# Attention and a two-product layer on one core: from whole batches in turn to 384-token chunks in a pipeline

## The chip, the cores and the metric

The kernel runs on one core of one Trainium2 chip. The metric is the device time of one execution in microseconds (us), lower is better. Before the change three runs gave 482.09 us (median), 481.46 and 484.16 us.

## The reference

Causal attention over 4 batches, 8 heads, 768 tokens and 64 numbers per head. Three heads (0, 2 and 6, "retrieval") see every earlier token. The other five ("streaming") see the first 4 tokens (the sink) and the last 64. The heads' outputs, side by side, are rows of 512 numbers, and two products with a leaky ReLU between them follow.

```python
scores = scale * np.matmul(q, k.transpose(0, 1, 3, 2))
rel = pos[:, None] - pos[None, :]
causal = rel >= 0
in_win = (rel >= 0) & (rel < int(window))              # window = 64
stream_keep = causal & (is_sink | in_win)              # is_sink: pos < 4
mask = np.where(retr[0, :, 0, 0, None, None], full_mask, stream_mask)
scores = np.where(mask[None, :, :, :], scores, -1000000000.0)
a = np.exp(scores - np.max(scores, axis=-1, keepdims=True))
a = a / (np.sum(a, axis=-1, keepdims=True) + 1e-09)
x = np.matmul(a, v)             # then (4, 768, 8 * 64) -> (3072, 512)
h = x @ w_in                    # 512 x 2048
out = np.maximum(0.01 * h, h) @ w_out                  # 2048 x 512
```

All inputs and the output are float32.

## The kernel before, in words

One loop runs over the four batches of 768 tokens, and each batch goes through all its stages in turn. The tile framework's scheduler may move instructions of the next batch forward, as far as buffers allow.

**Weights.** Both matrices come in one DMA each of 4 MB, before most else, and ScalarE turns them into bf16 in one instruction each (L87, L92).

**Loads and transposes.** `qb`, `kb` and `vb` of a batch come in one DMA each (L111 to L113). ScalarE casts them to bf16 (L117, L125). Scores need the 64 numbers of a head on the partitions, so q and k are written to a bridge in DRAM (`qk_bridge`, L126) and read back by a transposing DMA (L130) as `qt` and `kt`. Two heads share a column of 128 partitions, 64 each.

**Attention**, head by head. For a retrieval head the scores of a block of 128 keys against all later queries go to PSUM (`psST`, L152, weights of 64 rows), ScalarE takes the exponential (`At`, L156), VectorE masks the diagonal block (L162), and TensorE multiplies with `vpad` (L166, 65 columns: 64 of v and one of ones, whose sum is the denominator). A streaming head does the same in blocks of 128 x 128 for the diagonal and for the block before it (L185, L190, L194, L198) and a product with 4 rows for the sink. A head's sums stay in `psO`, six banks of PSUM, in one buffer; L214 and L215 copy them out.

**Second bridge.** The whole batch is normalised at once (L220), written to DRAM (`x_bridge`, L227) and read back transposed as `xt` (L229).

**Both products**, for 512 and then 256 tokens: for each of 16 groups of 128 hidden columns four matmuls with `w_in_bf` (`psH`, L239), the leaky ReLU on ScalarE (`gT`, L245), and one matmul with `w_out_bf` per 128 tokens (`psOUT`, L249). L253 copies the result out, and one DMA per batch stores it (L254).

So TensorE runs attention of a batch, then its products, then attention of the next.

## Time and profile before

| | |
|---|---|
| median of 3 runs | 482.09 us |
| span of the profiled execution | 482.3 us |
| TensorE matmul busy | 316.1 us, 66% |
| ScalarE busy | 193.2 us, 40% |
| VectorE busy | 90.8 us, 19% |
| GpSimd busy | 13.9 us, 3% |

The profiled execution left no time besides its span, which is its first to its last instruction, and the span is 0.2 us above the median: nothing of note lies around it. PE is TensorE, PEld its weight load, ACT ScalarE, DVE VectorE, POOL GpSimd, SP the engine that issues the DMAs. A matmul's "mean ns of one" contains its latency: how fast matmuls follow each other is read from the starts of neighbouring rows of the timeline, or from n of them in a row as (time of the row - time of one) / (n - 1). [...] Before the first recorded change of the clock the rows show 1.00 throughout, also where TensorE had not run yet: the level of that stretch is read from the matmuls' spacing.

### The profile page before, as it was taken

To read this page: it belongs to the slowest core of one execution; us is meant where nothing else is said; L and a number is where in the kernel's file an instruction comes from. 1 tells how busy PE (TensorE), PEld (TensorE's weight loads), DVE (VectorE), ACT (ScalarE), POOL (GpSimd) and SP (SyncE) were. 2 spreads that over 40 slices of the span, in tenths; PEclk is the share of its full clock that TensorE was granted. 3 is DMA by queue.
4 is the path that set the end of the run, shared out by engine and by line. 5 is a ranking of instruction groups with operands and counts; after the bars stand their busy time and mean duration, and the time that the engine had idled before them with its cause. 6 is when DMAs were issued, how large, how long until landed. Compare 5 with 4: busy or idle time off the path is not lost.

```text
span 482.3 us, 4494 instructions
## 1 busy us (share of the span) xinstructions
PE 316.1 (66%) x1764; PEld 148.8 (31%) x1784; DVE 90.8 (19%) x234; ACT 193.2 (40%) x339; POOL 13.9 (3%) x22
## 2 busy tenths in 40 slices
PE   0000297720998888810999998807999889259992
PEld 0000044310334444400334444402345344124351
DVE  0000033350001043430001144330010433400011
ACT  1827165632435564520233465421333655012331
POOL 4000000020000000020000000020000000000000
PEclk9999999999999975555899965557999755559997
DMA  8999997189997030099000030192000300130003
GB/s 330 230 341 287 229 218 173 67 185 228 225 254 153 0 132 1 1 248 251 24 1 0 1 131 1 13 196 55 0 1 0 132 0 1 65 65 1 0 1 131
DMA packets 71029, 52.72 MB, mean 109 GB/s; under 512 B 37728, under 2 KB 65376, under 8 KB 70496
## 3 DMA queue, kind: packets, MB, share of 16 engines
q1 hardware_dynamic: 71008, 52.43, 43.5%
q8 instruction: 14, 0.23, 0.2%
q14 instruction: 7, 0.06, 0.0%
HBM read 27.26 MB, written 15.73 MB: 89 GB/s over the span
## 4 chain that ended last, share of the span: by engine, by line
PE 57%; DMA 20%; ACT 11%; issue 4%; DVE 3%; SPq 3%; ACTq 0%
PE psOUT L249 18%; PE psH L239 16%; PE psO L166 11%; PE psST L152 7%; DMA xt<-x_bridge 6%; DMA kb<-in_k_dram 5%; ACT At L190 5%; PE psST L185 5%; DMA x_bridge<-x_sb 4%; DMA qk_bridge<-tb 4%; ACT gT L245 3%; SPq L130 3%; DVE x_sb L220 1%; ACT tb L125 1%; ACT At L156 1%
## 5 line engine op out<-in xcount | busy, mean ns | idle before, releaser
L239 PE MATMUL psH<-xt,w_in_bf 128*128 128x512 bf16 (+1 forms) x508 | 102.2, 338 | 71.4 <-DMA xt<-x_bridge 69.8
L245 ACT ACTIVATE gT<-psH 128x512 bf16<-128x512 f32 (+1 forms) x128 | 62.0, 490 | 159.2 <-PE psH L239 154.3
L249 PE MATMUL psOUT<-w_out_bf,gT 128*128 128x512 bf16 x368 | 97.5, 391 | 7.1 <-ACT gT L245 4.9
L152 PE MATMUL psST<-qt,kt 64*128 64x512 bf16 (+4 forms) x116 | 45.3, 436 | 67.4 <-DMA kt<-qk_bridge 57.0
L239 PEld LDWEIGHTS <-w_in_bf 128*128 128x128 bf16 x512 | 51.2, 101 | 116.8 <-DMA xt<-x_bridge 70.4
L156 ACT ACTIVATE At<-psST 128x512 bf16<-128x512 f32 (+4 forms) x116 | 51.1, 472 | 46.0 <-PE psST L152 45.1
L166 PE MATMUL psO<-vpad,At 128*128 128x65 bf16 (+1 forms) x552 | 66.7, 234 | 2.9 <-DVE At L194 2.3
L253 DVE COPY out_sb<-psOUT 128x2048 f32<-128x2048 f32 (+1 forms) x8 | 14.1, 1758 | 233.6 <-PE psOUT L249 233.6
L166 PEld LDWEIGHTS <-At 128*128 128x128 bf16 (+1 forms) x552 | 37.9, 111 | 52.0 <-DVE At L162 18.9
L249 PEld LDWEIGHTS <-gT 128*128 128x128 bf16 x384 | 30.9, 99 | 59.0 <-ACT gT L245 35.3
L190 ACT ACTIVATE At<-psST 128x512 bf16<-128x512 f32 x80 | 32.7, 461 | 24.6 <-PE psO L166 13.3
L185 PE MATMUL psST<-qt,kt 64*128 64x128 bf16 x220 | 35.8, 288 | 8.7 <-ACT At L190 7.0
L152 PEld LDWEIGHTS <-kt 64*128 64x128 bf16 (+1 forms) x116 | 9.4, 97 | 74.0 <-DMA kt<-qk_bridge 57.0
L162 DVE TENSOR_TENSOR At<-At,m_caus 128x128 bf16<-128x128 bf16 x72 | 15.9, 225 | 86.0 <-ACT At L156 83.7
L185 PEld LDWEIGHTS <-kt 64*128 64x128 bf16 x220 | 19.8, 121 | 22.6 <-issue 18.8
L214 DVE COPY xu_sb<-psO 128x384 f32<-128x384 f32 x32 | 17.8, 558 | 44.2 <-PE psO L166 44.2
L116 POOL MEMSET vpad<- 128x3120 bf16 x4 | 10.8, 2698 | 301.6 <-PE psO L166 301.6
L117 ACT ACTIVATE vpad<-vb 128x3072 bf16<-128x3072 f32 x4 | 11.1, 2766 | 14.5 <-POOL vpad L116 14.5
L125 ACT ACTIVATE tb<-qb 128x3072 bf16<-128x3072 f32 x4 | 11.0, 2761 | 10.6 <-DMA qb<-in_q_dram 10.6
L220 DVE TENSOR_TENSOR x_sb<-xu_sb,linv 128x3072 bf16<-128x3072 f32 x4 | 13.4, 3358 | 0.1
L125 ACT ACTIVATE tb<-kb 128x3072 bf16<-128x3072 f32 x4 | 11.0, 2758 | 4.4 <-DMA kb<-in_k_dram 4.4
L87 ACT ACTIVATE w_in_bf<-wtmp 128x8192 bf16<-128x8192 f32 x1 | 7.0, 7029 | 11.5 <-DMA wtmp<-in_moe_w_in_dram 11.5
(26 smaller groups left out, 46.9 us busy)
## 6 DMA issues: line engine op xcount, KB each, us to landing
qk_bridge<-tb SPq DMA_DIRECT2D x8, 768.0 KB, 6.8
out_dram<-out_sb SPq DMA_DIRECT2D x4, 1536.0 KB, 5.9
wtmp<-in_moe_w_in_dram SPq DMA_DIRECT2D x1, 4096.0 KB, 12.8
wtmp<-in_moe_w_out_dram SPq DMA_DIRECT2D x1, 4096.0 KB, 18.2
...
qb<-in_q_dram SPq DMA_DIRECT2D x4, 0.2 KB, 11.7
...
```

The lines of the kernel that those rows point to most:

```text
L125: nc.scalar.activation(out=tb[:], in_=src[:], func=mybir.ActivationFunctionType.Copy)
L152: nc.tensor.matmul(psST[:krows, :ww], lhsT=kslab, rhs=Qth[:, qstart + off : qstart + off + ww], start=True, stop=True,)
L156: nc.scalar.activation(out=At[:krows, off : off + ww], in_=psST[:krows, :ww], func=mybir.ActivationFunctionType.Exp, scale=SM,)
L162: nc.vector.tensor_mul(At[:krows, :msk_end], At[:krows, :msk_end], msk[:krows, :msk_end])
L166: nc.tensor.matmul(psO[:, qi, : D + 1], lhsT=At[:krows, q_off : q_off + 128], rhs=Vph[:krows, kj, :], start=first[qi], stop=is_last,)
L185: nc.tensor.matmul(psST[:, i * 128 : i * 128 + 128], lhsT=Kth[:, kj * 128 : kj * 128 + 128], rhs=Qth[:, qi * 128 : qi * 128 + 128], start= ...
L190: nc.scalar.activation(out=At[:, g0 : g0 + len(grp), :], in_=psST[:, : len(grp) * 128], func=mybir.ActivationFunctionType.Exp, scale=SM,)
L214: nc.vector.tensor_copy(xu_sb[:, :, h, :], psO[:, :, :D])
L220: nc.vector.tensor_tensor(x_sb.rearrange("p cg (h d) -> p cg h d", h=H), xu_sb[:], linv.to_broadcast([128, NCG, H, D]), op=mybir.AluOpType ...
L239: nc.tensor.matmul(psH[:], lhsT=w_in_bf[:, fg, ng * 128 : ng * 128 + 128], rhs=xt[:, fg, tok0 : tok0 + T], start=(fg == 0), stop=(fg == NF ...
L245: nc.scalar.activation(out=gT[:], in_=psH[:], func=mybir.ActivationFunctionType.Prelu, alpha=0.01)
L249: nc.tensor.matmul(psOUT[:, tt, :], lhsT=gT[:, tt * 128 : tt * 128 + 128], rhs=w_out_bf[:, ng, :], start=(ng == 0), stop=(ng == NNG - 1),)
```

## The change

The program is rewritten. Tokens go in 8 chunks of 384, two per batch. The order of every engine is the order in which the code is written (`manual_schedule`).

- **Work lists.** `prep_slots`, `attention_slots`, `in_slots` and `out_slots` give lists of small pieces ("slots") of a chunk. `merge` issues them by turns: slots of chunk n's first product, of chunk n-1's second product and of chunk n+1's transposes and attention.
- **Order at the start.** Attention of chunk 0 alone, its first product alone, attention of chunk 1 alone, its first product alone; then the second product of chunk 0 with attention of chunk 2; from there for n = 2 to 6 three things together; then n = 7's first product with 6's second, and 7's second alone.
- **Transposes** of q, k and of the attention's output are bf16 matmuls against an identity into `pt` (one PSUM buffer) with a copy to SBUF behind them. Both DRAM bridges are gone.
- **Padded heads.** `kt` holds each head on all 128 partitions, zeros in the other head's half, so all matmuls have 128 rows. Streaming heads use windows of 128 keys per 64 queries; the sinks of all streaming heads share one product (`ksink`, `vs`).
- **Lag.** A unit's scores and exponential stand two slots ahead of its product with v.
- **Casts** of q, k and v move from ScalarE to GpSimd (chunk 0: k on VectorE, q on ScalarE); those of the weights go to VectorE and GpSimd in 16 pieces each, and weights are loaded in 8 DMAs of 1 MB. `vb` and `vs` are shifted copies of v, made by DMA within SBUF.
- **PSUM**: 2 buffers each for scores, `po` and `ph`; one each for `pt` and `py`.

What TensorE has in a row where products and attention meet. Before, at the end of a batch's attention (`psO` of the last head, then `psH` of the first hidden group):

```order
L166 LDWEIGHTS At_520
L166 MATMUL psO_502<-vpad_119,At_520 128x65
L166 LDWEIGHTS At_507
L166 MATMUL psO_502<-vpad_119,At_507 128x65
L239 LDWEIGHTS w_in_bf_105
L239 MATMUL psH_558<-xt_554,w_in_bf_105 128x512
```

Now, in the stage of n = 3, between two slots of the products (`ph` is the first product of chunk 3, `psS` and `po` are scores and sums of chunk 4):

```order
L350 LDWEIGHTS w_in_bf_113
L350 MATMUL ph_2060<-xt_1305,w_in_bf_113 128x384
L234 LDWEIGHTS kt0_99
L234 MATMUL psS_2066<-qt_1788,kt0_99 128x384
L198 LDWEIGHTS ats2_111
L198 MATMUL po_2071<-va0_101,ats2_111 128x65
```

Before, the two kinds meet once per batch; now a few matmuls of attention stand after every three or four of the products.

What SP issues at the start. Before, with the first batch's bridge in the sixth row:

```order
L86 DMA wtmp_107<-in_moe_w_in_dram 128x4x2048
L111 DMA qb_113<-in_q_dram 128x48x64
L112 DMA kb_114<-in_k_dram 128x48x64
L91 DMA wtmp2_110<-in_moe_w_out_dram 128x16x512
L113 DMA vb_115<-in_v_dram 128x48x64
L126 DMA qk_bridge<-tb_124 128x6x512
L126 DMA qk_bridge<-tb_128 128x6x512
L130 DMA_TRANSPOSE qt_122<-qk_bridge 128x4x768
```

Now, from the third quarter of `w_in` on (chunk 0 and two quarters stand ahead of these; `kf_419`, `qf_423`, `vf_427` are chunk 1, `kf_515` and its fellows chunk 2, `vb0` the shifted v of chunk 1):

```order
L73 DMA wf_381<-in_moe_w_in_dram 128x4x512
L73 DMA wf_393<-in_moe_w_in_dram 128x4x512
L67 DMA kf_419<-in_k_dram 128x8x64 x3
L67 DMA qf_423<-in_q_dram 128x8x64 x3
L67 DMA vf_427<-in_v_dram 128x8x64 x3
L73 DMA wf_435<-in_moe_w_out_dram 128x4x512
L73 DMA wf_465<-in_moe_w_out_dram 128x4x512
L67 DMA kf_515<-in_k_dram 128x8x64 x3
L67 DMA qf_519<-in_q_dram 128x8x64 x3
L67 DMA vf_523<-in_v_dram 128x8x64 x3
L153 DMA vb0_103<-va0_101 64x1560
```

The first of these waits until VectorE and GpSimd have cast the first quarter of `w_in`, and VectorE's half of that cast stands behind all of its work for the attention of chunk 0; everything below it waits with it.

The core of the diff (masks, buffers and the sink's scores are left out; removed lines stand in the listing above, a few as marks here):

```diff
-    for b in range(B):
...
-        for h in range(H):
...
-        nc.sync.dma_start(out=x_dram[b].rearrange("(cg p) f -> p cg f", p=128), in_=x_sb[:])
...
-        nc.sync.dma_start_transpose(out=xt[:], in_=x_dram[b])
...
-        CHUNKS = [(0, 512), (512, 256)]
...
+    ctx.enter_context(tc.manual_schedule())
...
+    ps = ctx.enter_context(tc.tile_pool(name="ps", bufs=2, space=bass.MemoryType.PSUM))
...
+    def load(n, what):
+        b, c = divmod(n, 2)
+        for nm in what:
+            t = rot.tile([128, 3, H, D], FP32, name=f"{nm}f", tag=f"{nm}f", bufs=2)
+            for g in range(3):
+                nc.sync.dma_start(out=t[:, g], in_={"q": qr, "k": kr, "v": vr}[nm][b, c, :, :, g])
+            stage[nm, n] = t
+    def load_w(which, i):
+        t = rot.tile([128, 4, 512], FP32, name="wf", tag="wf", bufs=2)
+        src = w_in_r[:, :, 512 * i : 512 * i + 512] if which == "in" else w_out_r[:, 4 * i : 4 * i + 4, :]
+        nc.sync.dma_start(out=t[:], in_=src)
+        stage[which, i] = t
+    load(0, "kqv")
+    load_w("in", 0)
+    load_w("in", 1)
...
+    def zeros(i):
+        nc.vector.memset(kt[i][64:128, :, 0, :], 0.0)
+        nc.vector.memset(kt[i][0:64, :, 1, :], 0.0)
...
+    def cast_chunk(n):
+        b, c = divmod(n, 2)
+        i = b % 2
+        for nm in "kq":
+            tb = rot.tile([128, 3, H, D], BF16, name=f"{nm}b", tag=f"{nm}b", bufs=2)
+            src = stage[nm, n]
+            for g in range(3):
+                if n == 0 and nm == "k":
+                    nc.vector.tensor_copy(tb[:, g], src[:, g])
+                elif n == 0:
+                    nc.scalar.activation(out=tb[:, g], in_=src[:, g], func=ACTF.Copy)
+                else:
+                    nc.gpsimd.tensor_copy(tb[:, g], src[:, g])
+            cast[nm, n] = tb
+        src = stage["v", n]
+        for g in range(3):
+            nc.gpsimd.tensor_copy(va[i][:, 3 * c + g, :, 0:D], src[:, g])
...
+            nc.sync.dma_start(out=vb[i][0:64, 0:2], in_=va[i][64:128, 0:2])
+            nc.sync.dma_start(out=vb[i][64:128, 0:2], in_=va[i][0:64, 1:3])
+        else:
+            nc.sync.dma_start(out=vb[i][0:64, 2:5], in_=va[i][64:128, 2:5])
+            nc.sync.dma_start(out=vb[i][64:128, 2:5], in_=va[i][0:64, 3:6])
...
+    def prep_slots(n):
+        b, c = divmod(n, 2)
+        i = b % 2
+        qts[n] = rot.tile([128, 4, CH], BF16, name="qt", tag="qt", bufs=2)
+        def one_pair(nm, p):
+            pt = ps.tile([128, 4, 128], BF16, name="pt", tag="pt", bufs=1)
+            tb = cast[nm, n]
+            for g in range(3):
+                nc.tensor.transpose(pt[:, g, :], tb[:, g, 2 * p : 2 * p + 2, :], ident[:])
+            if nm == "q":
+                nc.vector.tensor_copy(qts[n][:, p, :], pt[:, 0:3, :])
+                return
+            for hh in range(2):
+                r = slice(64 * hh, 64 * hh + 64)
+                nc.vector.tensor_copy(kt[i][r, p, hh, CH * c : CH * c + CH], pt[r, 0:3, :])
...
+        return [lambda nm=nm, p=p: one_pair(nm, p) for p in range(4) for nm in "kq"]
...
+        def retr_units(p, hh):
+            h = 2 * p + hh
+            if c == 0:
+                groups = [[(0, 0)], [(1, 128), (2, 256)]]
+            else:
+                groups = [[(kj, 0)] for kj in range(4)] + [[(4, 128), (5, 256)]]
...
+                def qk(grp=grp, box=box):
+                    s = score()
+                    a = rot.tile([128, CH], BF16, name="at", tag="at", bufs=5)
+                    off = 0
+                    for j, (kj, lo) in enumerate(grp):
+                        w = CH - lo
+                        nc.tensor.matmul(
+                            s[:, off : off + w], lhsT=kt[i][:, p, hh, 128 * kj : 128 * kj + 128],
+                            rhs=qt()[:, p, lo:CH], start=(j == 0), stop=(j == len(grp) - 1),
+                            skip_group_check=True)
+                        off += w
+                    nc.scalar.activation(out=a[:, 0:off], in_=s[:, 0:off], func=ACTF.Exp, scale=SM)
+                    off = 0
+                    for (kj, lo) in grp:
+                        if 128 * kj >= q0:
+                            nc.vector.tensor_mul(a[:, off : off + 128], a[:, off : off + 128], m_caus[:])
+                        off += CH - lo
+                    box[0] = a
...
+                def do_av(grp=grp, box=box):
+                    off = 0
+                    for (kj, lo) in grp:
+                        for qi in range(lo // 128, 3):
+                            o = off + 128 * qi - lo
+                            av(p, hh, qi, box[0][:, o : o + 128], va[i][:, kj, h, :], None,
+                               False)
...
+                a = ats[ats_i[0] % len(ats)]
+                ats_i[0] += 1
+                for m in range(6):
+                    gm = 6 * c + m
+                    k0 = 64 * max(gm - 1, 0)
                     nc.tensor.matmul(
+                        s[:, 64 * m : 64 * m + 64], lhsT=kt[i][:, p, hh, k0 : k0 + 128],
+                        rhs=qt()[:, p, 64 * m : 64 * m + 64], start=(m == 0), stop=(m == 5),
+                        skip_group_check=True)
+                av_ = a[:, :, 0:4:3, :]
+                nc.scalar.activation(
+                    out=av_, in_=s[:, 0:CH].rearrange("p (j e f) -> p j e f", j=3, e=2),
+                    func=ACTF.Exp, scale=SM)
+                m_ = (m_win0 if c == 0 else m_win).rearrange("p (j e) f -> p j e f", j=3)
+                nc.vector.tensor_mul(av_, av_, m_)
+                box[0] = a
...
+            def do_av():
+                a = box[0]
+                for j in range(3):
+                    t = 3 * c + j
+                    ve = va[i][:, 0, h, :] if t == 0 else vb[i][:, t - 1, h, :]
+                    av(p, hh, j, a[:, j, 0:2, :], ve, None, False)
+                    av(p, hh, j, a[:, j, 2:4, :], va[i][:, t, h, :], None, False)
...
+        def finish_pair(p):
+            for j in range(sink_lo // 128, 3):
+                av(p, None, j, at_sink[0][:, 128 * j : 128 * j + 128], vs[i][:, 2 * p : 2 * p + 2, :], None, False)
+            linv = rot.tile([128, 3, 2], FP32, name="linv", tag="linv", bufs=2)
+            nc.vector.reciprocal(linv[:], po[p][:, :, :, D])
+            xs = rot.tile([128, 3, 2, D], BF16, name="xs", tag="xs", bufs=2)
+            nc.vector.tensor_tensor(xs[:], po[p][:, :, :, 0:D], linv.to_broadcast([128, 3, 2, D]), op=ALU.mult)
+            return xs
+        def x_t(p, xs):
+            pt = ps.tile([128, 4, 128], BF16, name="pt", tag="pt", bufs=1)
+            for j in range(3):
+                nc.tensor.transpose(pt[:, j, :], xs[:, j], ident[:])
+            nc.scalar.activation(out=xts[n][:, p, :], in_=pt[:, 0:3, :], func=ACTF.Copy)
...
+        slots = []
+        LAG = 2
+        pend = {}
+        nu = len(units)
+        for t in range(nu + LAG + 2):
+            def slot(t=t):
+                if t in pend:
+                    x_t(*pend.pop(t))
+                if t < nu:
+                    units[t][0]()
+                u = t - LAG
+                if 0 <= u < nu and units[u][1] is not None:
+                    units[u][1]()
+                    if units[u][2] is not None:
+                        pend[t + 2] = (units[u][2], finish_pair(units[u][2]))
+            slots.append(slot)
...
+    def in_slots(n):
+        gs[n] = rot.tile([128, NG, CH], BF16, name="g", tag="g", bufs=2)
+        def tick(t):
+            ph = ps.tile([128, 512], FP32, name="ph", tag="ph", bufs=2)
+            for g in range(KG):
+                nc.tensor.matmul(ph[:, 0:CH], lhsT=w_in_bf[:, g, 128 * t : 128 * t + 128],
+                                 rhs=xts[n][:, g, :], start=(g == 0), stop=(g == KG - 1))
+            nc.scalar.activation(out=gs[n][:, t, :], in_=ph[:, 0:CH], func=ACTF.Prelu, alpha=0.01)
...
+    def out_slots(n):
+        counts = [[3, 3, 3, 3, 4], [3, 3, 3, 3, 4], [3, 3, 3, 3, 2, 2]]
+        slots = []
+        def part(tt, lo, hi):
+            if lo == 0:
+                py[n] = ps.tile([128, 512], FP32, name="py", tag="py", bufs=1)
+            for ng in range(lo, hi):
+                nc.tensor.matmul(py[n][:], lhsT=gs[n][:, ng, 128 * tt : 128 * tt + 128],
+                                 rhs=w_out_bf[:, ng, :], start=(ng == 0), stop=(ng == NG - 1))
+            if hi == NG:
+                o = rot.tile([128, DM], FP32, name="o", tag="o", bufs=3)
+                nc.vector.tensor_copy(o[:], py[n][:])
+                r0 = CH * n + 128 * tt
+                nc.sync.dma_start(out=out[r0 : r0 + 128, :], in_=o[:])
+        for tt in range(3):
+            lo = 0
+            for w in counts[tt]:
+                slots.append(lambda tt=tt, lo=lo, w=w: part(tt, lo, lo + w))
+                lo += w
+        return slots
...
+    def cast_w(which, i):
+        t = stage[which, i]
+        for g in range(4):
+            dst = w_in_bf[:, g, 512 * i : 512 * i + 512] if which == "in" else w_out_bf[:, 4 * i + g, :]
+            if g < 2:
+                nc.vector.tensor_copy(dst, t[:, g, :])
+            else:
+                nc.gpsimd.tensor_copy(dst, t[:, g, :])
...
+    def merge(ms, as_):
+        na, nm = len(as_), len(ms)
+        done = 0
+        for j, m in enumerate(ms):
+            want = (j + 1) * na // nm if nm else na
+            while done < want:
+                as_[done]()
+                done += 1
+            m()
+        while done < na:
+            as_[done]()
+            done += 1
...
+    cast_chunk(0)
+    for f in prep_slots(0) + attention_slots(0):
+        f()
+    cast_w("in", 0)
+    load_w("in", 2)
+    zeros(1)
+    ins0 = in_slots(0)
+    def with_weights(t):
+        def f():
+            if t == 0:
+                cast_w("in", 1)
+                load_w("in", 3)
+            if t == 4:
+                load(1, "kqv")
+                cast_w("in", 2)
+                load_w("out", 0)
+            if t == 8:
+                cast_w("in", 3)
+                load_w("out", 1)
+            ins0[t]()
+        return f
+    for t in range(NG):
+        with_weights(t)()
+    load(2, "kqv")
+    cast_chunk(1)
+    for f in prep_slots(1) + attention_slots(1):
+        f()
+    ins1 = in_slots(1)
+    for t in range(NG):
+        if t in (4, 8, 12):
+            cast_w("out", t // 4 - 1)
+            if t < 12:
+                load_w("out", t // 4 + 1)
+        ins1[t]()
+    cast_w("out", 3)
+    load(3, "kqv")
+    cast_chunk(2)
+    merge(out_slots(0), prep_slots(2) + attention_slots(2))
+    for n in range(2, NCH):
+        a = []
+        if n + 1 < NCH:
+            if n + 2 < NCH:
+                load(n + 2, "kqv")
+            cast_chunk(n + 1)
+            a = prep_slots(n + 1) + attention_slots(n + 1)
+        merge(weave(in_slots(n), out_slots(n - 1)), a)
+    for f in out_slots(NCH - 1):
+        f()
...
```

## Rows read from the trace of the kernel before

**Rows 1.** The page: TensorE's granted clock, tenths, in 40 slices of the span.

```profile
PEclk9999999999999975555899965557999755559997
```

**Rows 2.** Stretches by stage: start:end, length, busy per engine, clock, DMA share, GB/s.

```profile
core 0: us, PE busy (x) PEld busy (x) DVE busy (x) ACT busy (x) POOL busy (x), PEclk, DMA share, GB/s
0.00:57.00 57.00, 0.00 (x0) 0.00 (x0) 0.45 (x2) 23.62 (x6) 5.78 (x19) 1.00 1.02 285
57.00:70.00 13.00, 11.61 (x68) 4.96 (x69) 4.38 (x16) 7.25 (x17) 0.00 (x0) 1.00 1.08 225
...
168.00:207.00 39.00, 33.95 (x226) 16.67 (x226) 16.23 (x54) 21.31 (x50) 0.30 (x1) 0.60 0.15 47
...
176.00:178.00 2.00, 2.00 (x15) 1.05 (x14) 0.49 (x2) 0.68 (x2) 0.00 (x0) 0.50 0.04 11
207.00:228.40 21.40, 0.00 (x0) 0.00 (x0) 4.05 (x4) 2.77 (x1) 2.39 (x1) 0.50 1.11 257
228.40:274.50 46.10, 44.45 (x216) 20.44 (x222) 2.29 (x1) 15.28 (x32) 0.00 (x0) 0.94 0.04 13
475.00:482.30 7.30, 0.00 (x0) 0.00 (x0) 0.00 (x0) 0.00 (x0) 0.00 (x0) 0.57 0.58 217
```

**Rows 3.** Waits: engine line <- whom: us in total, times, longest.

```profile
PE psH L239 <- DMA xt<-x_bridge: 69.8, 4, 21.9
PE psST L152 <- DMA kt<-qk_bridge: 57.0, 1, 57.0
```

**Rows 4.** The chain that ended last, shares of the span by engine.

```profile
PE 57%; DMA 20%; ACT 11%; issue 4%; DVE 3%; SPq 3%; ACTq 0%
```

**Rows 5.** Timeline of PE, first product stage: start us, us, line, out<-in, count.

```profile
122.09 1.89 PE L249 MATMUL psOUT<-w_out_bf,gT 128*128 128x512 bf16 x4
123.77 1.83 PE L239 MATMUL psH<-xt,w_in_bf 128*128 128x512 bf16 x6
125.43 1.89 PE L249 MATMUL psOUT<-w_out_bf,gT 128*128 128x512 bf16 x8
127.16 1.89 PE L239 MATMUL psH<-xt,w_in_bf 128*128 128x512 bf16 x8
```

**Rows 6.** Timeline of PE, second batch's attention, around the fall of the clock.

```profile
171.10 0.51 PE L166 MATMUL psO<-vpad,At 128*128 128x65 bf16 x11
...
174.33 0.38 PE L185 MATMUL psST<-qt,kt 64*128 64x128 bf16 x4 [0.47 <-ACT At L190]
...
175.86 1.84 PE L166 MATMUL psO<-vpad,At 128*128 128x65 bf16 x14
...
178.43 0.51 PE L166 MATMUL psO<-vpad,At 128*128 128x65 bf16 x6
```

**Rows 7.** Groups of the page: xcount | busy us, mean ns | idle before, releaser.

```profile
L156 ACT ACTIVATE At<-psST 128x512 bf16<-128x512 f32 (+4 forms) x116 | 51.1, 472 | 46.0 <-PE psST L152 45.1
L166 PE MATMUL psO<-vpad,At 128*128 128x65 bf16 (+1 forms) x552 | 66.7, 234 | 2.9 <-DVE At L194 2.3
...
L190 ACT ACTIVATE At<-psST 128x512 bf16<-128x512 f32 x80 | 32.7, 461 | 24.6 <-PE psO L166 13.3
```

**Rows 8.** Groups by line and shape, columns as above.

```profile
L185 PE MATMUL psST<-qt,kt 64*128 64x128 bf16 x220 | 35.8, 288 | 8.7 <-ACT At L190 7.0 <-ACT At L156 1.7
...
L214 DVE COPY xu_sb<-psO 128x384 f32<-128x384 f32 x32 | 17.8, 558 | 44.2 <-PE psO L166 44.2
...
L116 POOL MEMSET vpad<- 128x3120 bf16 x4 | 10.8, 2698 | 301.6 <-PE psO L166 301.6
...
L198 DVE TENSOR_TENSOR At<-At,m_sprev 128x512 bf16<-128x512 bf16 x20 | 8.5, 426 | 0.0
...
L156 ACT ACTIVATE At<-psST 128x384 bf16<-128x384 f32 x12 | 5.9, 489 | 2.0 <-PE psST L152 2.0
...
L253 DVE COPY out_sb<-psOUT 128x1024 f32<-128x1024 f32 x4 | 4.9, 1224 | 55.6 <-PE psOUT L249 55.6
...
L58 POOL TENSOR_SCALAR_AFFINE_SELECT m_caus<-m_caus 128x128 bf16<-128x128 bf16 x1 | 0.3, 293 | 0.0
```

More of the change, by code (lines that the diff above doesn't have):

```diff
@@ new lines @@
+    DM = moe_w_in.shape[0]
+    DF = moe_w_in.shape[1]
+    NG = DF // 128
+    KG = DM // 128
+    NCH = B * (S // CH)
+    ctx.enter_context(tc.manual_schedule())
+    one = ctx.enter_context(tc.tile_pool(name="one", bufs=1))
+    rot = ctx.enter_context(tc.tile_pool(name="rot", bufs=2))
+    ps = ctx.enter_context(tc.tile_pool(name="ps", bufs=2, space=bass.MemoryType.PSUM))
+    qr = q.rearrange("b h (c g p) d -> b c p h g d", g=3, p=128)
+    kr = k.rearrange("b h (c g p) d -> b c p h g d", g=3, p=128)
@@ new lines, in load_w @@
+    def load_w(which, i):
[6 more added lines that the diff above has]
+    load_w("in", 1)
+    ident = one.tile([128, 128], BF16, name="ident")
+    make_identity(nc, ident)
+    m_caus = one.tile([128, 128], BF16, name="m_caus")
+    nc.gpsimd.memset(m_caus[:], 1.0)
@@ new lines @@
+    nc.gpsimd.affine_select(
+        out=m_caus[:], in_=m_caus[:], compare_op=ALU.is_ge, fill=0.0,
+        base=0, channel_multiplier=-1, pattern=[[1, 128]],
+    )
+    m_win = one.tile([128, 6, 64], BF16, name="m_win")
+    nc.gpsimd.memset(m_win[:], 1.0)
+    nc.gpsimd.affine_select(
+        out=m_win[:], in_=m_win[:], compare_op=ALU.is_gt, fill=0.0,
+        base=0, channel_multiplier=1, pattern=[[0, 6], [-1, 64]],
+    )
+    nc.gpsimd.affine_select(
+        out=m_win[:], in_=m_win[:], compare_op=ALU.is_ge, fill=0.0,
+        base=64, channel_multiplier=-1, pattern=[[0, 6], [1, 64]],
+    )
@@ new lines @@
+    m_win0 = one.tile([128, 6, 64], BF16, name="m_win0")
+    nc.vector.tensor_copy(m_win0[:, 2:], m_win[:, 2:])
+    nc.vector.tensor_copy(m_win0[:, 0, :], m_caus[:, 0:64])
+    nc.vector.tensor_copy(m_win0[:, 1, :], m_win[:, 1, :])
+    nc.vector.memset(m_win0[0:NS, 1, :], 1.0)
+    kt = [one.tile([128, 4, 2, S], BF16, name=f"kt{i}") for i in range(2)]
+    va = [one.tile([128, 6, H, D + 1], BF16, name=f"va{i}") for i in range(2)]
+    vb = [one.tile([128, 5, H, D + 1], BF16, name=f"vb{i}") for i in range(2)]
@@ new lines @@
+    vs = [one.tile([128, H, D + 1], BF16, name=f"vs{i}") for i in range(2)]
+    ksink = [one.tile([128, 4, 128], BF16, name=f"ksink{i}") for i in range(2)]
+    ats = [one.tile([128, 3, 4, 64], BF16, name=f"ats{i}") for i in range(4)]
+    w_in_bf = one.tile([128, KG, DF], BF16, name="w_in_bf")
+    w_out_bf = one.tile([128, NG, DM], BF16, name="w_out_bf")
+    def zeros(i):
+        nc.vector.memset(kt[i][64:128, :, 0, :], 0.0)
+        nc.vector.memset(kt[i][0:64, :, 1, :], 0.0)
+        nc.gpsimd.memset(ksink[i][:], 0.0)
+        nc.gpsimd.memset(va[i][:, :, :, D], 1.0)
+        nc.gpsimd.memset(vs[i][:], 0.0)
@@ new lines @@
+    zeros(0)
+    for a in ats:
+        nc.gpsimd.memset(a[:, :, 1:3, :], 0.0)
+    cast = {}
+    qts = {}
+    def cast_chunk(n):
[16 more added lines that the diff above has]
+        if c == 0:
+            for h in range(H):
+                if not IS_RETR[h]:
+                    nc.sync.dma_start(out=vs[i][4 * h : 4 * h + NS, h, :], in_=va[i][0:NS, 0, h, :])
+            nc.sync.dma_start(out=vb[i][0:64, 0:2], in_=va[i][64:128, 0:2])
[3 more added lines that the diff above has]
+            nc.sync.dma_start(out=vb[i][64:128, 2:5], in_=va[i][0:64, 3:6])
@@ new lines, in prep_slots @@
+    def prep_slots(n):
[14 more added lines that the diff above has]
+                h = 2 * p + hh
+                if c == 0 and not IS_RETR[h]:
+                    nc.gpsimd.tensor_copy(ksink[i][r, p, 4 * h : 4 * h + NS], kt[i][r, p, hh, 0:NS])
+        return [lambda nm=nm, p=p: one_pair(nm, p) for p in range(4) for nm in "kq"]
@@ new lines @@
+    gs = {}
+    py = {}
+    def in_slots(n):
[6 more added lines that the diff above has]
+            nc.scalar.activation(out=gs[n][:, t, :], in_=ph[:, 0:CH], func=ACTF.Prelu, alpha=0.01)
+        return [lambda t=t: tick(t) for t in range(NG)]
@@ new lines, in out_slots @@
+    def out_slots(n):
[17 more added lines that the diff above has]
+                lo += w
+        return slots
@@ new lines, in weave @@
+    def weave(a, b):
+        r = []
+        for x, y in zip(a, b):
+            r += [x, y]
+        return r
+    cast_chunk(0)
[19 more added lines that the diff above has]
+        return f
```

250 lines of the change are left out of this document (64 added, 186 removed).

## The prediction

> **What bounds the kernel now.** I read the stretches by stage first, then the waits, then the timeline of TensorE.
>
> The stages stand one behind the other [rows 2]. Up to 57 us TensorE does nothing: weights, q, k and the first bridge are fetched (DMA share 1.02). From the second batch on, a batch is attention (39.0 us, TensorE busy for 34.0), a gap with no matmul while the second bridge is written and read (21.4 us there), and both products (46.1 us). The waits say the same: 57.0 us for `kt` and 69.8 us, in four pieces, for `xt` [rows 3], together 127 us in which TensorE stands still. On the chain that ended last TensorE has 57%, DMA 20%, ScalarE 11% [rows 4].
>
> The second loss is the clock. Products run at 0.94 of the full clock, attention at 0.60 on the mean and at 0.50 from about 176 us [rows 2]; in the slices it is at 5 in every later attention and gap [rows 1]. What that costs is in the starts of the timeline: at the low level 4 matmuls of 512 columns take 123.77 - 122.09 = 1.68 us, 420 ns each, at the high level 8 take 127.16 - 125.43 = 1.73 us, 216 ns each [rows 5]. So a column costs 0.82 or 0.42 ns. The first of these rows also show that the clock was low in the first attention, where the slices print 9.
>
> Attention is a chain at either level: 116 + 80 = 196 exponentials [rows 7] are 49 per batch, and 39.0 us by 49 is 0.80 us per exponential with what hangs on it, while the instruction itself takes 0.49 us for 384 columns [rows 8].
>
> **The change, part by part.** The columns of the products are the same. Both bridges go, and with them the 127 us of waits; in their place come transposes on TensorE, a start that is still serial, and a pipeline.
>
> *TensorE's work per chunk at the high level.* Products: 64 matmuls of 384 columns (162 ns by column) and 48 of 512 (216 ns), 10.4 + 10.4 = 20.7 us. Attention: 65 columns cost (0.51 - 0.23) / 10 = 28 ns [rows 6, 7], and 128 columns 54 ns by column (at most 0.38 / 4 = 95 ns [rows 6]). An even chunk has 36 transposes (1.9), 2304 columns of retrieval scores (1.0), 30 streaming scores of 64 (0.8), 1024 sink columns (0.4), 48 products with v (1.3) and 8 for the sink (0.4): 6.0 us. An odd chunk sees twice the keys: 1.9 + 2.4 (5760 columns) + 0.8 + 0.65 + 2.1 + 0.7 = 8.6 us. Padding the heads adds no columns. It may even help: 14 products with v of a streaming head, among them the sink's with 4 rows, take 1.84 us, 124 ns each, where 6 of a retrieval head at the same low clock take (0.51 - 0.23) / 5 = 56 ns [rows 6].
>
> *Stalls in the pipeline.* `pt` has one buffer. A k pair holds it for three transposes, two copies of 0.5 us (0.56 for the like copy [rows 8]) and handovers, 1.35 us, a q pair 0.95 us; between two such slots lies one product slot of 0.65 us beside 0.16 us of transposes. That leaves 0.5 + 0.1 us, four times: 2.5 us per chunk. A unit's chain (matmul end 0.2, exponential 0.49, often behind a leaky ReLU of the same size, mask 0.35 by the 0.43 for 512 columns [rows 8], handovers) is 1.6 to 2 us against about 1.8 us of other work in two slots; I take 0.2 us a unit, 12 or 21 units: 2.4 or 4.2 us. Bounds: nothing, or the 0.80 us in full, which is a rival below. ScalarE has 32 or 41 instructions of 0.49 us per chunk, at most 20 us, and GpSimd 9 casts, neither of which fills 31 us. So a chunk in the pipeline takes 26.7 + 4.9 = 31.6 us with an even and 29.3 + 6.7 = 36.0 us with an odd neighbour.
>
> *The start.* A third of a chunk's load is 0.79 MB, 3.5 us at the 225 GB/s that loads of q, k and v had alone [rows 2]; with some 2 us of latency (bounds: 0, and the 7.3 us in which 1.6 MB were stored at the end) k is there at 5.5, q at 9, v at 12.5 us. q is cast at 10. Transposes alone, low clock: 1.65 us for a k pair, 1.1 for a q pair, 11 us in all, so to 19.5. Then 12 units of 0.80 us and a tail of 3 us (last sums, transposes, copy): attention of chunk 0 ends at 32.
>
> Its first product needs `w_in` in bf16, and VectorE casts only now: 1 us, then 10.4 us and 2.5 us for a low clock at its head, as the first product stage of before had from 122.09 on [rows 5]: 46. Behind that cast SP has two quarters of `w_in`, then chunk 1: 2.1 + 1.6 MB at 250 to 285 GB/s, so q of chunk 1 lands near 49.5 and GpSimd has cast it at 50.5. A GpSimd cast of 512 columns is not in the trace; 0.44 us by the memset (2698 ns for 3120) and 1.17 by four times the mask's 293 ns for 128 [rows 8] bound it, I take 0.8, halfway. Transposes of chunk 1 end at 60, 21 units and a tail at 80. The shifted v of chunk 1 is needed at about 66 and stands on SP behind half of `w_out` and all of chunk 2, 8.9 MB after 33 us, so 69: 3 us more, 83. First product: 96. Half of `w_out` and then q and k of chunk 2 pass through GpSimd's queue, ten casts, 2 us of which are left over: 98. Second product of chunk 0 with attention of chunk 2: 10.4 + 6.0 + 4.9, and 1.7 for the slots that outnumber it: 121.
>
> *The rest.* n = 2 to 6: 3 x 36.0 + 2 x 31.6 = 171.2, so 292. Chunk 7 alone with 6's second product 21.2, so 313.5. The last second product 10.4 us and twice 1.0 us, because `py` has one buffer and its copy (half of 1.22 [rows 8]) lies bare: 326. Last copy 0.6 us and a store of 0.26 MB, between 0 and the 7.3 us of 1.6 MB [rows 2], I take 4: 331 us. The span of before is its time, so no more is added.
>
> [...]
>
> **The rivals.**
>
> *Chains bound the pipeline.* If interleaving hid nothing, a chunk would be 20.7 us and, for attention, 11 + 12 x 0.80 + 3 = 23.6 or 30.8 us: 44.3 or 51.5. Over n = 2 to 6 that is 243 instead of 171, and 11 more in the stage before: 414 us. For it: one `pt`, ScalarE shared by exponentials and ReLUs in strict order. Against: a lag of two slots and products between. Half hidden: 373 us.
>
> *The start comes late.* Three joins (chunk 1's casts, its shifted v, chunk 2's casts) hang on one SP queue and one GpSimd queue. Seven us more at each is 352 us.
>
> *A transpose costs its latency.* One matmul of 128 columns took 288 ns on its own [rows 8]; 288 of these less the 54 ns charged: 67 us more, 398 us. Against: four in a row ended in 0.38 us [rows 6].
>
> *The clock stays low* (the other side). In the attention of before TensorE was busy for 34 of 39 us and had 0.50 all the same [rows 2], and the pipeline is full of such short matmuls. At 0.82 ns per column the products of a chunk take 40.3 us, attention 11.7 or 16.9. n = 2 to 6 is then 3 x 63.9 + 2 x 56.9 = 305.5, 134 more; the two first products alone add 15, the stage before the pipeline 14, the last two 19 and 10: 523 us, slower than before. It decides from 151 / 192 = 78% of that time at the low level. Against: over two thirds of TensorE's time in the pipeline are the products' long matmuls, and in a run of those the clock rose [rows 5]. [...] In the products of before, which do wait for ScalarE, the mean was 0.94 [rows 2].
>
> **How the numbers follow.** Forecast 331 us, 0.60, its own range 312 to 352; start late 0.10; chains 0.15; latency of transposes 0.04; low clock 0.06 (two thirds of it past the point from which it is slower); fewer stalls than taken, under 312, 0.05. The low end takes away all stalls of the five chunks, 28 us: 302. The high end is the half hidden chain with most of a late start: 390. About 15 in 100 is left out. A change under 0.5% (2.4 us) could not be told from none here. Faster 0.95, within 0.01, slower 0.04.
>
> **What would show it.** Attention of chunk 0 ends near 32 us, of chunk 1 near 83; first weights of `w_out` enter TensorE near 98. From there the granted clock is 0.9 or more, ScalarE and VectorE are busy for about half, and chunks alternate between 32 and 36 us. `pt` is waited for in the first third of each chunk, 2 to 3 us. Wrong it would be if the clock fell in the transposes' slots, if matmuls of `po` waited for masks by more than 0.5 us each, or if TensorE waited for GpSimd's casts after n = 2.

## The result, and the profile after

The changed kernel takes 321.11 us (median of four runs, 319.85 to 321.69), the kernel before took 482.93 us beside it (481.46 to 484.16): a ratio of 0.665, with a 95% interval of 0.663 to 0.667. The forecast was 331 us.

Of the page of the changed kernel, the granted clock in 40 slices and the shares of the chain that ended last; they answer to [rows 1] and [rows 4]:

```profile
PEclk9996796758599999999997999999999999999999
...
PE 47%; DMA 16%; DVE 13%; SPq 12%; issue 4%; POOL 4%; ACT 2%; POOLq 0%; ACTq 0%
```

From the twelfth slice on the clock is high, with one dip. 28% of the chain is still DMA and SP's queue, and the waits of TensorE, which answer to [rows 3], say where:

```profile
PE po L198 <- DMA vb<-va: 17.2, 5, 9.4
PE pt L165 <- DVE kt L171: 11.0, 25, 0.9
...
PE po L198 <- DVE at L243: 0.6, 2, 0.3
```

The 127 us that TensorE waited for bridges are gone. The largest wait is a new one, 17.2 us in five pieces for `vb`, the shifted copy of v. Waits of `po` for masked scores, which the forecast feared, come to 0.6 us for `at` and as much for `ats`.

The stretches by stage, columns as in [rows 2]. They are: attention of chunk 0; its first product; transposes and attention of chunk 1; its first product; second product of chunk 0 with attention of chunk 2; n = 2 to 6 of the pipeline; n = 7; the last second product and the store.

```profile
0.00:32.00 32.00, 14.49 (x137) 9.52 (x138) 16.64 (x45) 10.35 (x20) 11.44 (x33) 0.91 0.66 148
32.00:45.40 13.40, 13.31 (x66) 6.86 (x64) 5.64 (x8) 7.76 (x17) 5.03 (x7) 0.83 1.01 247
45.40:83.40 38.00, 18.01 (x175) 11.76 (x176) 11.44 (x37) 11.17 (x26) 6.05 (x10) 0.70 0.72 159
83.40:96.80 13.40, 13.40 (x69) 7.09 (x68) 3.08 (x7) 8.02 (x17) 6.95 (x11) 0.83 1.03 262
96.80:119.80 23.00, 18.41 (x180) 10.12 (x183) 13.27 (x37) 7.47 (x17) 7.32 (x17) 1.00 0.39 78
119.80:151.60 31.80, 30.19 (x282) 18.19 (x284) 12.82 (x37) 18.14 (x41) 5.60 (x9) 1.00 0.58 113
151.60:184.60 33.00, 29.33 (x247) 17.55 (x251) 13.03 (x38) 15.15 (x34) 6.18 (x14) 0.95 0.54 105
184.60:217.60 33.00, 30.20 (x283) 18.18 (x284) 13.05 (x37) 18.14 (x41) 5.55 (x9) 1.00 0.55 108
217.60:249.20 31.60, 27.78 (x247) 16.88 (x251) 13.08 (x38) 15.16 (x34) 6.38 (x14) 1.00 0.54 109
249.20:280.60 31.40, 30.00 (x283) 18.12 (x285) 12.54 (x37) 18.01 (x41) 0.00 (x0) 1.00 0.12 39
280.60:302.20 21.60, 21.14 (x111) 10.91 (x112) 2.08 (x3) 8.05 (x18) 0.00 (x0) 1.00 0.10 37
302.20:319.70 17.50, 10.95 (x48) 4.58 (x47) 2.77 (x4) 0.26 (x1) 0.00 (x0) 1.00 0.16 60
```

Two things are to be seen. Attention with twice the keys (n = 2, 4 and 6, an odd chunk) does not cost more than attention of an even chunk (n = 3 and 5): TensorE has 30 us to do in the one and 28 to 29 in the other, and all five take 31.4 to 33.0 us. And the only mean clock under 1.00 after 96.8 us is in the stage from 151.6 on. The timeline of TensorE there (columns as in [rows 5]) shows both at one place:

```profile
165.70 0.81 PE L350 MATMUL ph<-xt,w_in_bf 128*128 128x384 bf16 x4
166.35 0.33 PE L234 MATMUL psS<-qt,kt 128*128 128x256 bf16 x2
...
169.57 0.20 PE L198 MATMUL po<-vb,ats 128*128 128x65 bf16 x1 [2.83 <-DMA vb<-va]
...
171.13 1.49 PE L350 MATMUL ph<-xt,w_in_bf 128*128 128x384 bf16 x4
172.41 0.53 PE L269 MATMUL psS<-qt,kt 128*128 128x64 bf16 x6
```

Before the wait, 4 matmuls of 384 columns take 166.35 - 165.70 = 0.65 us; behind 2.83 us without a matmul the same 4 take 172.41 - 171.13 = 1.28 us, the low level. A pause alone doesn't decide it: two stages later TensorE stood still for longer, and the clock of that stage is 1.00 throughout.

```profile
235.84 0.20 PE L198 MATMUL po<-vb,ats 128*128 128x65 bf16 x1 [3.08 <-DMA vb<-va]
```

SP's timeline (same columns; SPq is issuing) shows why `vb` is late, here one stage of the pipeline:

```profile
218.83 2.00 SPq L67 DMA_DIRECT2D kf<-in_k_dram  x3
...
224.25 4.86 SPq L67 DMA_DIRECT2D vf<-in_v_dram  x3
229.22 3.35 SPq L149 DMA_DIRECT2D vs<-va  x5
232.66 0.52 SPq L150 DMA_DIRECT2D vb<-va  x1
```

The code issues the loads of chunk n + 2 ahead of the shifted copies of chunk n + 1. SP spends 10 us on those loads, and `vb`, needed in this stage, is issued at 232.66; this is the copy that TensorE waited for until 235.84.

### The profile page after: what moved, and what is told of

Read it like the earlier page. It is cut to its first block, busy times and chain, and to the rows that moved or that the text cites. A ratio compares the mean times of both kernels' runs of the same rounds, so it can differ in the third digit from the quotient of the medians.

```text
span 319.7 us, 5340 instructions
## 1 busy us (share of the span) xinstructions
PE 257.2 (80%) x2107; PEld 149.8 (47%) x2136; DVE 119.4 (37%) x323; ACT 137.7 (43%) x296; POOL 60.5 (19%) x123
## 4 chain that ended last, share of the span: by engine, by line
PE 47%; DMA 16%; DVE 13%; SPq 12%; issue 4%; POOL 4%; ACT 2%; POOLq 0%; ACTq 0%
PE py L364 18%; PE ph L350 11%; SPq L67 11%; DMA vb<-va 6%; PE po L198 5%; DMA qf<-in_q_dram 5%; DMA vf<-in_v_dram 4%; PE pt L165 3%; DVE kt L171 3%; DVE o L368 3%; PE psS L234 3%; PE pt L303 2%; DVE xs L297 2%; PE psS L269 2%; DMA wf<-in_moe_w_out_dram 2%
## 5 line engine op out<-in xcount | busy, mean ns | idle before, releaser
L350 PE MATMUL ph<-xt,w_in_bf 128*128 128x384 bf16 x512 | 106.0, 339 | 0.1
L364 PE MATMUL py<-w_out_bf,g 128*128 128x512 bf16 x355 | 97.0, 381 | 4.0 <-DVE o L368 2.3
L352 ACT ACTIVATE g<-ph 128x384 bf16<-128x384 f32 x128 | 63.0, 492 | 82.9 <-PE ph L350 82.4
L239 ACT ACTIVATE at<-psS 128x384 bf16<-128x384 f32 x84 | 40.5, 492 | 23.0 <-PE psS L234 22.3
L364 PEld LDWEIGHTS <-g 128*128 128x128 bf16 x384 | 33.6, 98 | 27.7 <-issue 5.3
L171 DVE COPY kt<-pt 64x384 bf16<-64x384 bf16 x64 | 22.7, 355 | 20.4 <-PE pt L165 19.8
L234 PE MATMUL psS<-qt,kt 128*128 128x384 bf16 (+2 forms) x108 | 29.4, 315 | 0.8 <-ACT at_sink L214 0.4
L198 PE MATMUL po<-vb,ats 128*128 128x65 bf16 x100 | 11.9, 199 | 17.6 <-DMA vb<-va 17.2
L198 PE MATMUL po<-va,at 128*128 128x65 bf16 x252 | 23.5, 203 | 0.8 <-DVE at L243 0.6
L304 ACT ACTIVATE xt<-pt 128x384 bf16<-128x384 bf16 x32 | 15.7, 490 | 15.9 <-PE pt L303 15.6
L278 DVE TENSOR_TENSOR ats<-ats,m_win 128x384 bf16<-128x384 bf16 x40 | 14.9, 372 | 16.3 <-ACT ats L274 16.1
L274 ACT ACTIVATE ats<-psS 128x384 bf16<-128x384 f32 x40 | 19.2, 490 | 3.9 <-PE psS L269 3.7
L297 DVE TENSOR_TENSOR xs<-po,linv 128x384 bf16<-128x384 f32 x32 | 17.8, 558 | 1.1
```

The lines of the kernel that those rows point to most:

```text
L171: nc.vector.tensor_copy(kt[i][r, p, hh, CH * c : CH * c + CH], pt[r, 0:3, :])
L198: nc.tensor.matmul(o, lhsT=lhsT, rhs=rhs, start=first, stop=last, skip_group_check=True)
L234: nc.tensor.matmul(s[:, off : off + w], lhsT=kt[i][:, p, hh, 128 * kj : 128 * kj + 128], rhs=qt()[:, p, lo:CH], start=(j == 0), stop=(j == ...
L239: nc.scalar.activation(out=a[:, 0:off], in_=s[:, 0:off], func=ACTF.Exp, scale=SM)
L274: nc.scalar.activation(out=av_, in_=s[:, 0:CH].rearrange("p (j e f) -> p j e f", j=3, e=2), func=ACTF.Exp, scale=SM)
L297: nc.vector.tensor_tensor(xs[:], po[p][:, :, :, 0:D], linv.to_broadcast([128, 3, 2, D]), op=ALU.mult)
```

## The experiments

Times that stand with a range are medians of four runs with an interval against the kernel before, the others single runs. A stage is one n of the pipeline.

### The shifted v ahead of the next loads

Theory: `vb` is late only for its place in SP's order. Rival: it is late whatever its place (bandwidth, the casts).

```diff
-    load(2, "kqv")
     cast_chunk(1)
+    load(2, "kqv")
...
-            if n + 2 < NCH:
-                load(n + 2, "kqv")
             cast_chunk(n + 1)
+            if n + 2 < NCH:
+                load(n + 2, "kqv")
```

> The loads of chunk n+2 are issued behind the shifted copies of v of chunk n+1 (chunks 1 and 3 to 7) instead of ahead of them. In the trace of the changed kernel TensorE waits 17.2 us for these copies: 9.4 us in the attention of chunk 1 and 0.5 + 2.8 + 1.4 + 3.1 = 7.8 us in the stages of n = 2 to 5, and the clock falls once behind one of them (3.4 us at the low level, worth 1.7). Theory: these waits are SP's order alone. They go, and nothing takes their place: 321 - 17.2 - 1.7 = 302 us. Rival: the copies wait for GpSimd's cast of v or take that long themselves, and the loads behind them now come late for the next chunk's casts: 315 us or more, with a wait of TensorE for GpSimd's casts in the stages.

302.37 us (301.86 to 302.99), ratio 0.624 (0.623 to 0.626): 18.7 us less than the changed kernel. SP's timeline at the start, and the stretches from the second product of chunk 0 on:

```profile
52.69 0.48 SPq L153 DMA_DIRECT2D vb<-va  x1
...
54.33 7.29 SPq L67 DMA_DIRECT2D kf<-in_k_dram  x3
```

```profile
85.90:110.00 24.10, 19.08 (x182) 10.45 (x187) 13.50 (x37) 7.38 (x17) 9.44 (x21) 1.00 0.48 94
110.00:141.30 31.30, 30.20 (x282) 18.18 (x284) 12.28 (x38) 18.30 (x41) 5.56 (x9) 1.00 0.58 114
141.30:169.60 28.30, 27.56 (x247) 16.80 (x250) 13.16 (x38) 14.91 (x33) 6.48 (x14) 1.00 0.56 122
```

`vb` is issued at 52.69 instead of 65.04, TensorE waits for it nowhere, the dip of the clock is gone, and even stages are now shorter than odd ones: 28.3 against 31.3 us. The pipeline begins 96.8 - 85.9 = 10.9 us earlier, the rest comes off its stages. The theory holds; this is also the second of the forecast's three joins, seen alone.

### The pipeline without interleaving

Theory: the gain has two halves, the bridges and the interleaving, and without the second a chunk costs its products plus its attention. `merge` issues all of one chunk's products first, and then the attention:

```diff
-            want = (j + 1) * na // nm if nm else na
+            want = 0
```

> Slots of the products and of attention are no longer issued by turns: in each stage all product slots come first, then transposes and attention of the next chunk. Theory (interleaving hides attention's chain and keeps the clock up): attention alone takes what it took in the two serial chunks of the changed kernel, 22.6 us for an even and some 26 us for an odd chunk, and 2 us of low clock stand at the head of every product stage: 3 x 49 + 2 x 45.5 = 238 us for n = 2 to 6 instead of 161, 12 us more in the stage before: 321 + 89 = 410 us, granted clock 0.5 in the attention stretches. Rival (the gain is the bridges and the waits for them, interleaving brings little, as TensorE's own work sets the time): attention costs TensorE's 6 to 9 us and the stalls of a stage: under 345 us.

410.17 us. An odd chunk's attention, the products behind it and an even chunk's attention:

```profile
155.20:180.70 25.50, 15.58 (x178) 10.03 (x177) 11.34 (x35) 10.92 (x26) 0.00 (x0) 0.85 0.64 114
180.70:203.20 22.50, 21.91 (x110) 11.28 (x112) 1.38 (x2) 7.99 (x17) 0.00 (x0) 0.94 0.07 24
203.20:226.60 23.40, 14.11 (x137) 9.96 (x136) 13.63 (x35) 7.23 (x17) 11.57 (x23) 0.59 0.67 131
```

Of 161.8 us (482.9 to 321.1), 72.8 came with the bridges' going and all else of the rewrite, which no run takes apart, and 89.1 with interleaving. Alone, attention has TensorE busy for 14 or 15.6 of 23.4 or 25.5 us. Among products it adds some 6 or 9 us to the 22.5 of products alone: stages take 28.3 or 31.3 us once `vb` is out of the way (the run above). The time was as expected; the clock was not. It was expected at 0.5 in these attentions and was 0.85 in one and 0.59 in the other, so the part of the loss that belongs to the clock is smaller than the theory had it.

Nor is the rest the chain of single units, from scores over exponential and mask to the product with v. TensorE's largest waits in this run are those of the transposes:

```profile
PE pt L165 <- DVE kt L171: 28.9, 31, 1.4
PE pt L303 <- DVE xs L297: 25.0, 32, 1.3
```

In the changed kernel they are 11.0 and 6.7 us. Over the whole run the waits for k and q copies out of `pt` (28.9 and 10.8 us) and for the normalised sums `xs` (25.0) come to 64.7 us, those for masked scores to 2.6 us. So, with a lag of two slots, TensorE's idle time in attention alone lies mostly at the one buffer of the transposes and the copies around it.

### Every transpose twice

Theory: a transpose costs its 128 columns, 54 ns. Rival: its latency, 233 to 239 ns by the groups of the changed kernel ("mean ns of one").

```diff
-            for g in range(3):
+            for g in [0, 1, 2] * 2:
...
-            for j in range(3):
+            for j in [0, 1, 2] * 2:
```

> Every transpose on TensorE is issued twice (288 more matmuls of 128 columns). Theory (a transpose costs its columns): 216 in the pipeline at 54 ns and 72 in the two serial chunks at 107 ns, 11.7 + 7.7 = 19 us more at most, 333 to 340 us. Rival (each costs its latency of 0.24 to 0.29 us): 69 to 83 us more, 390 to 404 us.

327.84 us, 6.7 more, less than either expected. Part of the cost was hidden: waits for `vb` fell from 17.2 to 9.2 us, since what is issued before them came later. The last full stage has no such wait in either kernel:

```profile
254.20:287.30 33.10, 31.76 (x313) 20.03 (x317) 12.22 (x38) 18.38 (x41) 0.00 (x0) 1.00 0.12 38
```

33.1 against 31.4 us, so 1.7 us for 36 more transposes, 47 ns each. The rival falls: a "mean" of 0.24 us is what one takes from start to end, and the next starts long before that. The clock stayed at 1.00 through this stage, which had 72 of them.

### Scores with 64 rows, as before

Theory: padded heads spare TensorE a change between 64 and 128 rows at each turn from scores to products with v. Rival: padding is worth nothing.

```diff
-   lhsT=kt[i][:, p, hh, ...],                      rhs=qt()[:, p, ...]
+   lhsT=kt[i][64 * hh : 64 * hh + 64, p, hh, ...], rhs=qt()[64 * hh : 64 * hh + 64, p, ...]
```

(in the scores of retrieval heads and of the windows; the sinks stay).

> Scores read the 64 rows of their head alone instead of 128 with zeros; columns and instructions stay. Theory (a change between matmuls of 64 and 128 rows costs about 0.1 us, as the spacing between the two kinds in the attention of before suggests): 93 units in the pipeline change twice, 93 x 2 x 0.1 = 18 us more, about 338 us. Rival (padding is neutral, the slow products with v of before had another cause): 320 to 323 us.

335.74 us, 14.6 more. The same last full stage, and TensorE's timeline at two units, first of this kernel, then of the changed one:

```profile
259.60:295.20 35.60, 34.19 (x282) 17.11 (x284) 12.55 (x38) 18.26 (x41) 0.00 (x0) 1.00 0.11 35
```

```profile
275.70 0.33 PE L234 MATMUL psS<-qt,kt 64*128 64x384 bf16 x1
275.97 0.27 PE L198 MATMUL po<-va,at 128*128 128x65 bf16 x3
276.16 0.33 PE L234 MATMUL psS<-qt,kt 64*128 64x384 bf16 x1
```

```profile
264.11 0.33 PE L234 MATMUL psS<-qt,kt 128*128 128x384 bf16 x1
264.27 0.26 PE L198 MATMUL po<-va,at 128*128 128x65 bf16 x3
264.36 0.32 PE L234 MATMUL psS<-qt,kt 128*128 128x384 bf16 x1
```

From the start of a score to the next product with v it is 0.27 instead of 0.16 us, and from three such products to the next score 0.19 instead of 0.09. There are 40 such changes in this stage, and (35.6 - 31.4) / 40 is 0.105 us each. The columns are the same, a score takes 0.33 us in both, and the wait for `pt` is 1.2 us in both stages, so this is the price of changing between 64 and 128 rows. The traces don't show what the time goes into.

### A lag of one slot

On the kernel with `vb` first, to see how much of a unit's chain the lag of two slots covers.

```diff
-        LAG = 2
+        LAG = 1
```

> On the kernel with the copies of v first (302.4 us): a unit's product with v stands one slot behind its scores instead of two. Theory (the chain matmul end 0.2, exponential 0.49, mask 0.27 to 0.37, handovers 0.2 is some 1.2 us; two slots of other work cover it, one of 0.65 us plus the next scores does not): 0.3 us for each of 99 units in the pipeline and for the 33 serial ones, 40 us more, 330 to 345 us. Rival (the chain is far shorter than the forecast took it, since no unit waited with a lag of two): under 310 us.

317.94 us, 15.6 more than with two, between the theory and its rival. Waits of the weight load for the scores of a unit, with a lag of one and then of two:

```profile
PEld L198 <- DVE at L243: 10.1, 25, 0.8
PEld L198 <- ACT at L239: 9.9, 21, 1.0
```

```profile
PEld L198 <- DVE at L243: 2.5, 7, 0.5
```

With two the view lists none for the exponential. TensorE's own waits for `at` and `ats` are 10.4 us in all with one and 1.3 with two.

First transposes of three chunks in a row, the lag of one and then of two:

```profile
116.19 0.33 PE L165 MATMUL pt<-ident,kb 128*128 128x128 bf16 x3
...
150.40 0.27 PE L165 MATMUL pt<-ident,kb 128*128 128x128 bf16 x2
...
179.14 0.33 PE L165 MATMUL pt<-ident,kb 128*128 128x128 bf16 x3
```

```profile
109.57 0.33 PE L165 MATMUL pt<-ident,kb 128*128 128x128 bf16 x3
...
141.70 0.27 PE L165 MATMUL pt<-ident,kb 128*128 128x128 bf16 x2
...
169.16 0.33 PE L165 MATMUL pt<-ident,kb 128*128 128x128 bf16 x3
```

34.2 and 28.7 us instead of 32.1 and 27.5: 2.1 us for 21 units and 1.3 us for 12, some 0.1 us a unit. 6 us of the 15.6 lie before the pipeline, where attention stands alone. So within the pipeline the chain is longer than one slot by about 0.1 us, and two slots cover it with room. That is why the stall of 0.2 us a unit, which the forecast took with two, was not there.

### The start in the pipeline too

On the kernel with `vb` first: chunk 1's attention is merged with chunk 0's first product, so only attention of chunk 0 stands alone. All loads of the weights and of chunks 1 and 2 are issued before it, and GpSimd casts the weights. Two small changes go with it: masks and zeros are made in another order, and the middle tile of the last product uses a buffer of `ph`.

```diff
-    for f in prep_slots(1) + attention_slots(1):
-        f()
...
+    for f in attention_slots(0):
+        f()
+    merge(in_slots(0), prep_slots(1) + attention_slots(1))
...
-    for n in range(2, NCH):
+    for n in range(1, NCH):
```

> On the kernel with the copies of v first: the first product of chunk 0 is interleaved with attention of chunk 1, and of chunk 1 with the second product of chunk 0 and attention of chunk 2. For that all loads of chunks 1 and 2 and of the weights are issued earlier, GpSimd alone casts the weights, as they land, VectorE clears its buffers before the first masks, and the middle tile of the last product uses another bank. Theory (what is left of the start is serial work, not data): attention of chunk 0 ends at 31, the next stage takes 26 us (attention's chain), then three stages of 28 and three of 31 us, 21 and 13 for the last products, 4 at the end: 275 to 280 us. Rival (15.5 MB of loads, or 23 us of weight casts on GpSimd, then hold the second stage back): 285 us or more, with TensorE waiting for casts between 55 and 70 us.

283.27 us (282.21 to 283.6), ratio 0.585 (0.584 to 0.587): the fastest of all, 37.8 us under the changed kernel (18.7 of these by `vb`), and 3 us above what was expected. The merged stage of chunk 0 and the one behind it:

```profile
35.30:65.50 30.20, 26.26 (x235) 16.18 (x234) 11.60 (x32) 17.06 (x41) 15.15 (x26) 1.00 0.98 258
65.50:93.70 28.20, 27.45 (x247) 16.77 (x250) 12.67 (x37) 15.14 (x33) 10.96 (x22) 1.00 0.67 145
```

The merged stage was expected at 26 us and took over 30. Its clock stands as 1.00 only because no change was recorded before it: 4 matmuls of 384 columns took 45.05 - 43.77 = 1.28 us at 43.77 and 0.65 us at 46.42, so the level rose at about 46 us, and a third of the stage ran at the low one. From 65 us on the stages are those of the kernel with `vb` first. Of the rival, waits for the loads and casts, two pieces appeared: 1.0 us for `vb` and 0.9 us for a cast, once each. Of the 19.1 us under the kernel with `vb` first, 16.3 had come by the start of the first stage with an odd chunk (93.7 instead of 110.0); the `ph` buffer for the last product shows in the waits for its copy, 0.8 instead of 2.3 us.

### Half of the k copies on ScalarE

On the last kernel: the copy of a k pair's second head goes from VectorE to ScalarE, so that both run side by side and `pt` comes free earlier.

```diff
-                nc.vector.tensor_copy(kt[i][r, p, hh, ...], pt[r, 0:3, :])
+                if hh == 0:
+                    nc.vector.tensor_copy(kt[i][r, p, hh, ...], pt[r, 0:3, :])
+                else:
+                    nc.scalar.activation(out=kt[i][r, p, hh, ...], in_=pt[r, 0:3, :], func=ACTF.Copy)
```

> The kernel with the merged start, and ScalarE takes one of the two copies of each k pair out of the transposes' buffer. Theory (VectorE's two copies of 0.35 us in a row hold the buffer): 0.35 us less for each of 32 pairs where it is waited for, 3 us in the serial chunk and the chain-bound stage and 3 to 5 us in the pipeline: 6 to 8 us less. Rival (ScalarE then starts exponentials later): no change or up to 5 us more.

287.39 us (286.43 to 288.19), ratio 0.594 (0.592 to 0.596): 4 us slower instead of 6 to 8 faster. ScalarE's waits:

```profile
ACT kt L178 <- DVE kt L176: 26.2, 25, 1.9
```

Ahead of 25 of its 32 copies ScalarE stood idle until VectorE's had ended. They write different parts of the same tile `kt` and read different parts of `pt`; here the second was still ordered behind the first, and the trace doesn't tell for which of the two tiles. So they ran one behind the other, TensorE's wait for `pt` behind k copies grew from 10.8 to 16.3 us, and the run doesn't test the theory: what a shorter hold of `pt` would be worth stays open.

## Why the forecast came out

By its own terms, in us of the span:

| term | forecast | measured |
|---|---|---|
| attention of chunk 0 ends | 32 | 32.0 |
| its first product ends | 46 | 45.4 |
| attention of chunk 1 ends | 83 | 83.4 |
| its first product ends, first `w_out` | 96, 98 | 96.8, 96.5 |
| out0 with attention of chunk 2 | 23 | 23.0 |
| three stages with an odd chunk | 108.0 | 96.2 |
| two stages with an even chunk | 63.2 | 64.6 |
| n = 7 with 6's second product | 21.2 | 21.6 |
| last product and store | 17.5 | 17.5 |
| around the span | 0 | 1.7 |

- *What bounds it* held. The bridges' waits are gone, and with interleaving the clock is 1.00 but for one dip. The run without merging puts interleaving at 89.1 us, and the bridges with all else of the rewrite at 72.8. What it corrects is the picture of attention as a chain of units: alone, in the new order, it waits for transposes.
- *The start* was right in its sum. The wait for `vb` in chunk 1's attention, taken at 3 us, was 9.4, since TensorE came to it at 61.1 instead of 66: transposes had ended at 56.1 instead of 60. The copy itself was there at 70.5 instead of 69, and as all else waited for it, the earlier transposes could only lengthen the wait. The forecast had named SP's place of that copy and reached its 69 by counting bytes; in the trace SP issues chunk 2's nine loads for 15 us ahead of it (49.80 to 64.94), and with the copy ahead of them the wait is gone.
- *Stalls in the pipeline* were sized too high: for an odd chunk 6.7 us taken, about 2 found (31.4 less the 29.3 of column work), for an even one 4.9 taken, 1.6 found with `vb` out of the way (28.3 less 26.7). The larger part is the unit's chain, 0.2 us a unit taken against nothing found; the run with a lag of one shows the chain at one slot and 0.1 us. The rest is `pt`: the k copies were taken at 0.5 us,

```profile
L171 DVE COPY kt<-pt 64x384 bf16<-64x384 bf16 x64 | 22.7, 355 | 20.4 <-PE pt L165 19.8
...
L141 POOL CAST kb<-kf 128x512 bf16<-128x512 f32 x21 | 12.4, 614 | 40.1 <-DMA kf<-in_k_dram 39.9
L386 POOL CAST w_out_bf<-wf 128x512 bf16<-128x512 f32 x8 | 5.6, 725 | 35.1 <-DMA wf<-in_moe_w_out_dram 35.1
```

  by these groups of the changed kernel they are 0.355. The GpSimd cast, taken at 0.8 us halfway between far bounds, is 0.61 to 0.73.
- *What was missing* is the wait for `vb` in the pipeline: 0.51, 2.83, 1.40 and 3.08 us, 7.8 in all, and some 2 us more by the clock behind the second of them. It took the place of the stalls in even stages, which without it are 28.3 us. The forecast looked for this copy at the start alone; SP's order is the same in each stage.
- *Luck.* Without these waits the five stages take 150.9 us (the run with `vb` first), where the forecast had 171.2: 20 us too many, of which the copy gave 10 back. The kernel that the forecast describes, but for its 3 us for `vb` at the start, is that run's, and its 302.4 us lie under the 312 where the forecast's own range begins. So the mechanism was right, and part of the nearness of 331 to 321 is two errors that cancel.
- *Rivals.* Chains as the bound is near the time of the run without merging, 410 us beside the 414 worked out, so interleaving is what keeps it away. The parts agree less well: attention of an odd chunk took 25.5 us, not 30.8, and products 22.5, not 20.7. The late start came in one of its three joins, `vb`. Latency of transposes fell (47 ns). The low clock did not come: stages full of short matmuls stood at 1.00, with pauses of up to 0.7 us for `pt` in them. The one fall in the pipeline stood behind a pause of 2.83 us, and a pause of 3.08 us brought none.
- *Sums.* Two are slightly off, and neither moves the forecast: the parts of an even chunk's attention add up to 5.8 us, not 6.0, and the stalls of the five chunks to 29.9, not 28.
- *Signs.* `pt` is waited for in the first third of a stage, for 0.4 to 1.2 us and not 2 to 3. ScalarE is busy for 15 to 18 us of 32, VectorE for 13, about half and less. The alternation of 32 and 36 us was not there: it was hidden by `vb`, and with it out of the way it is 28.3 and 31.3 to 31.6.
